# Gate and up in blocks of 128 features in both layers, and w_down in smaller pieces

## The chip, the cores and the metric

The kernel runs on one core of a Trainium2 chip. The metric is the device time of one execution in microseconds (us). Before the change three runs took 646.38, 647.87 and 648.17 us, median 647.87. The profile is of one further execution, which took 647.37 us.

The engines are named as in the profile: PE (matrix engine; PEld are its loads of the stationary operand), DVE, ACT, POOL, and SP, which here only issues transfers (DMA).

## The reference

One token for each of B = 4 sequences passes through two layers. Each layer is a block of attention over a cache and a feed-forward block, both on a normalised x and both added to x. The same caches and weights serve both layers.

```
x: [4, 1, 512]   k_cache, v_cache: [4, 8, 8192, 128]   wq: [512, 4096]   wo: [4096, 512]
w_gate, w_up: [512, 1792]   w_down: [1792, 512]          all bf16

twice:
  h = layernorm(x)
  q = h @ wq                      # 32 heads of 128; 4 query heads share one of 8 KV heads
  p = softmax(q k^T / sqrt(128))  # over 8192 keys
  x = x + (p v) @ wo
  h = layernorm(x)
  x = x + (silu(h @ w_gate) * (h @ w_up)) @ w_down
```

K and V are 64 MB each and are read in both layers, apart from a few pieces that are kept. With the weights, read in each layer or once, 271 MB come in.

## The kernel before, in words

**Tiles and slots.** One tile of K or V is 4 MB: two KV heads of one sequence, all 8192 keys, 32 KB on each of 128 partitions. `kvf` holds five slots of that size. `todo` runs over the 16 pairs of a layer: `keys` turns K by transposes on DVE (L581) and multiplies it with the queries (L607), `values` multiplies V with the probabilities (L745). All transfers go through SP in the order of the list `cmds`; `freed` marks places of a slot as free and `pump` issues the next transfers of the list as long as their place is free. Nothing else decides the order.

**Weights of the feed-forward block.** When attention nears its end, a slot that is free takes the weights (`W_SLOT`: slot 1 in layer 0, slot 3 in layer 1). w_gate has 4 passes of 128 input features (kt), each 1792 features wide; w_up the same, part of it in a place that stays for both layers. w_down is cut into ranges of 128-feature blocks, `WDS[L]`: five ranges in layer 0, three in layer 1. In layer 0 there is too little room: two ranges have a place (one in `pT`), and the other three go where gate passes 0, 1 and 2 were, each issued when its pass has been multiplied (`freed(s, NB + 2 + k, ...)`). In layer 1 two ranges are issued with gate and up, the third, blocks 12 and 13, when the last pair's probabilities (`late`) are no longer needed.

**Gate and up.** `ffn(L)` does gate in bank `gb`, then up in bank `ub`, pass by pass (wg0 to wg3, wu0 and wu1), and a small matmul for the variance (`deviation`, L931) after gate pass 1. The two layers differ:

- Layer 0: x is stationary (4 columns), the weights stream by. Each pass has four strips of FW = 448 features (`strips`), one for each quarter of the array, so that the results of sequence b lie on partitions 0, 32, 64 and 96 plus b. One strip of up is cut in two where its weights lie in two places: 33 matmuls in all. `on_end` (L1023) turns each bank by a transpose on DVE, and features come to lie on partitions. Feature p x 14 + f is then on partition p, and w_down is loaded to match: partition p holds rows p x 14 + f.
- Layer 1: the weights are stationary, 128 features a block, x streams by (4 columns): 14 blocks a pass, 112 in all. Results have features on partitions at once. `base(fo)` gives a block's first feature and the step between its features, so that they match the order in which w_down lies: for range j in groups of `WDE[j]` rows, a partition holds `WDE[j]` consecutive rows. `WDE = (8, 4, 2)`: the blocks of range 0 take every 8th feature, those of range 1 every 4th, of range 2 every 2nd.

**From there** DVE and ACT compute gate times its sigmoid (L1054 to L1060, the rstd of the norm is multiplied in) and times up (L1062), which gives hT in bf16. In layer 0 w_down follows with its blocks stationary (L1079), range by range as they land; in layer 1 hT is stationary and w_down streams by into four quarters of a bank (L1069), so that the result is in rows and can go out (L1144, L1146, L1148). `x_rows` (L907) adds x into the same bank. L912 to L926 (`center`) stand ahead of both: mean, xn, squares.

**Queries.** `qproj` (L996) uses quarters of the array as layer 0's gate and up do. The change leaves it as it is.

Of the kernel before, what the change touches and what calls it, by code (L numbers as in the profile page):

```python
# [6 lines left out]
ALU = mybir.AluOpType  # L7
# [96 lines left out]
def bass_interleave_layers__gqa_block_cached__swiglu_ffn__decode_kernel(  # L104
# [18 lines left out]
    P = 128  # L123
# [21 lines left out]
    with ExitStack() as es:  # L145
# [14 lines left out]
        WDS = (((12, 14), (10, 12), (0, 2), (2, 6), (6, 10)), ((0, 8), (8, 12), (12, 14)))  # L160
        WDE = (8, 4, 2)
        NW = max(len(w) for w in WDS)
# [24 lines left out]

        def base(fo):
            j = next(j for j, w in enumerate(WDS[1]) if w[0] <= fo < w[1])
            a, e = WDS[1][j][0], WDE[j]  # L190
            return a * P + (fo - a) // e * e * P + (fo - a) % e, e

        FW = F // NA
        assert FW * NA == F and FW == FO * QB and FW <= 512

# [4 lines left out]
        def wu_at(s, k, f, n, e=1):  # L200
            o = k * F + f
            o = (NSLOT + 1) * SL + o if o < RES else s * SL + O_WU + o - RES
            return kvf[:, o:o + e * (n - 1) + 1:e]

        def strips(up, k):
            for a in range(NA):
                cuts = [a * FW, (a + 1) * FW]
                if up and cuts[0] < RES - k * F < cuts[1]:
                    cuts.insert(1, RES - k * F)
                for f, end in zip(cuts, cuts[1:]):  # L210
                    yield a, f, end - f

# [270 lines left out]
        def load_wd(w0, L, j, also=()):  # L483
            a, b = WDS[L][j]
            o = 0 if w0 is pTf else wd_from(L, a)
            dst, src = w0[:, o:o + (b - a) * D], B_w_down.rearrange("(p f) n -> p (f n)", f=FO)[:, a * D:b * D]
            if L:
                dst = dst.rearrange("p (m x) -> p m x", x=WDE[j] * D)
                src = B_w_down[a * P:b * P, :].rearrange("(m p e) n -> p m (e n)", p=P, e=WDE[j])
            T.dma("sp", dst, src, sem_w["wd"][j], writes=[f"wd{j}"] + list(also))  # L490

# [519 lines left out]
        def ffn(L):  # L1011
# [3 lines left out]
            uT = bank(ub)[:, 0:FO * B]  # L1015
            fb = lambda ap: ap.rearrange("p (f b) -> p b f" if L else "p (b f) -> p b f", b=B)
            rb = rstd[:].unsqueeze(2).to_broadcast([P, B, FO])

            def on_end(k):
                if L:  # L1020
                    return
                blk = bank(k)[:, 0:FW].rearrange("p (i f) -> p f i", f=FO)
                T.op("dve", lambda e: e.transpose(blk, blk), reads=[f"pb{k}"], writes=[f"pb{k}"])  # L1023
            rooms = {"wg0": room(s, 0, F), "wg1": room(s, F, 2 * F), "wg2": room(s, 2 * F, 3 * F), "wg3": room(s, 3 * F, O_WU), "wu0": [], "wu1": room(s, O_WU, O_WD)}
# [4 lines left out]
            for wname, bk, ks in (("wg0", gb, (0, 1)), ("wg1", gb, (1, 2)),  # L1029
                                      ("wg2", gb, (2, 3)), ("wg3", gb, (3, KT)),  # L1030
                                      ("wu0", ub, (0, KT // 2)), ("wu1", ub, (KT // 2, KT))):
                at = wu_at if bk == ub else wg_at
                for kt in range(*ks):
                    parts = [(0, *base(fo), fo) for fo in range(FO)] if L else [(a, f, w, 0) for a, f, w in strips(bk == ub, kt)]
                    for n, (a, f, w, fo) in enumerate(parts):
                        x = xn[:, kt * B:(kt + 1) * B]
                        if L:
                            to, lhs, rhs = bank(bk)[:, fo * B:(fo + 1) * B], at(s, kt, f, P, w), x
                        else:
                            to, lhs, rhs = bank(bk)[a * QB:a * QB + B, f - a * FW:f - a * FW + w], x, at(s, kt, f, w)  # L1040
                        T.op("pe", lambda e: e.matmul(to, lhsT=lhs, rhs=rhs, start=(kt == 0 and fo == 0),  # L1041
                                                      stop=(kt == KT - 1 and (not L or fo == FO - 1))),
                             reads=rooms[wname] + names[wname] + ["xn"], writes=[f"pb{bk}"],
                             sig=(kt == ks[1] - 1 and n == len(parts) - 1))
                if wname in ("wg0", "wg1", "wg2"):
                    k = int(wname[2])
                    if not L:
                        freed(s, NB + 2 + k, NB + 3 + k)
                    if k == 1:
                        deviation(zero_sb, "zero", SBK[1])  # L1050
                elif wname != "wu0":
                    freed(s, *((0 if L else GATE, UP) if wname == "wg3" else (UP, DOWN)))
            on_end(gb)
            T.op("dve", lambda e: e.tensor_tensor(fb(gr), fb(gT), rb, ALU.mult),  # L1054
# [5 lines left out]
            T.op("dve", lambda e: e.tensor_tensor(eg, gw, eg, ALU.mult), reads=["gw", "eg"], writes=["eg"])  # L1060
            on_end(ub)
            T.op("dve", lambda e: e.tensor_tensor(hT.rearrange("p (f b) -> p b f", b=B), fb(eg), fb(uT), ALU.mult), reads=[f"pb{ub}", "eg"], writes=["hT"])  # L1062
            if L == 1:
# [114 lines left out]
```

## Time and profile before

| | |
|---|---|
| median of three runs | 647.87 us (646.38 to 648.17) |
| profiled execution | 647.37 us, span 645.1 us |
| PE busy | 414.8 us (64%) |
| PE weight loads busy | 172.3 us (27%) |
| DVE busy | 426.3 us (66%) |
| ACT, POOL busy | 50.2 us (8%), 11.9 us (2%) |
| DMA | 271.76 MB, mean 421 GB/s; queue 1: 98.8% of 16 engines |
| mean granted clock of PE | 0.841 |

How to read it: shares are of the span. The span is cut into 40 slices of 16.1 us; a digit is the busy share in tenths. Timeline lines give start and duration in us, engine, line of the kernel, operation, operands and how many instructions were merged; in brackets stands the idle time before and what ended it. A merged line's duration is from the first start to the last end, so that overlapping instructions are not counted twice. "DMA to landing" is the time from a transfer's issue to the arrival of its last part. The profiled execution's own time is 2.24 us more than its span.

### The profile page before, as it was taken

Reading aid. Unit: us, or ns where it says so; the run is one execution under the profiler, and the core shown is the slowest. Engines: PE = TensorE matmul, PEld = TensorE weight load, DVE = VectorE, ACT = ScalarE, POOL = GpSimd, SP = SyncE. Lnnn points to the kernel's source line nnn. Section 1 sums busy time; section 2 is a strip of 40 time slices with the busy share of each in tenths; the row PEclk is TensorE's granted clock in tenths of the full one; section 3 lists DMA queues with packets and bytes.
Section 4 is the critical chain, followed back from the end, with each engine's and each line's share of the span. In section 5 each row is a group of like instructions: output and inputs, shape, how many; then the busy total and the mean of one; then the engine's idle time right before and its main releaser. Section 6 shows DMA issues by size and latency. Waiting matters only on the chain.

```text
span 645.1 us, 6824 instructions
## 1 busy us (share of the span) xinstructions
PE 414.8 (64%) x2807; PEld 172.3 (27%) x2809; DVE 426.3 (66%) x599; ACT 50.2 (8%) x138; POOL 11.9 (2%) x44
## 2 busy tenths in 40 slices
PE   0583475457765746757856977667655567657867
PEld 0231122122222312322223332222222222223326
DVE  5375467456776656777853878967765557766953
ACT  0100000000000000000010300000000000000110
POOL 0000000000000000000000000000000000000000
PEclk9995887688876888778975999998777897679986
DMA  9999999999999999999999999999999999999995
GB/s 367 446 422 419 445 430 423 426 431 440 427 425 440 430 427 430 433 433 426 435 411 372 415 441 425 432 430 437 426 433 430 433 426 431 439 426 428 439 409 218
DMA packets 15502, 271.76 MB, mean 421 GB/s; under 512 B 1640, under 2 KB 1648, under 8 KB 6896
## 3 DMA queue, kind: packets, MB, share of 16 engines
q1 hardware_dynamic: 15472, 271.33, 98.8%
q8 instruction: 22, 0.36, 0.2%
q14 instruction: 8, 0.07, 0.0%
HBM read 271.32 MB, written 0.00 MB: 421 GB/s over the span
## 4 chain that ended last, share of the span: by engine, by line
DMA 60%; DVE 20%; PE 15%; issue 4%; ACT 0%; SPq 0%; POOL 0%; ACTq 0%; DVEq 0%; POOLq 0%
DMA kvf<-in_A_k_cache_dram 45%; DVE kvf L581 15%; DMA kvf<-in_A_v_cache_dram 11%; PE ps L607 8%; DMA kvf<-in_A_wq_dram 3%; PE ps L745 2%; DVE pb L797 2%; PE ps L1041 1%; DMA kvf<-in_B_w_down_dram 1%; PE ps L996 1%; DVE pT L673 1%; DVE pb L793 1%; DVE ps L547 0%; DVE scr L807 0%; PE ps L889 0%
## 5 line engine op out<-in xcount | busy, mean ns | idle before, releaser
L607 PE MATMUL ps<-kvf,zq 128*128 128x512 bf16 x1024 | 291.1, 430 | 186.0 <-DVE kvf L581 178.7
L581 DVE STREAM_TRANSPOSE kvf<-kvf 128x2048 f32<-128x2048 f32 (+1 forms) x133 | 280.5, 2132 | 125.4 <-DMA kvf<-in_A_k_cache_dram 125.2
L607 PEld LDWEIGHTS ps<-kvf,zq 128*128 128x128 bf16 x1024 | 98.7, 108 | 344.0 <-DVE kvf L581 223.6
L745 PE MATMUL ps<-kvf,pT 128*32 128x512 bf16 x960 | 65.8, 396 | 1.5 <-DVE pT L673 1.5
L655 ACT ACTIVATE pb<-ps,tiny 128x512 bf16<-128x512 f32 x32 | 24.9, 777 | 507.7 <-DVE tiny L653 489.2
L673 DVE STREAM_TRANSPOSE pT<-pb 64x512 bf16<-64x512 bf16 x60 | 41.2, 686 | 3.0 <-ACT pb L655 2.0
L797 DVE SCALAR_TENSOR_TENSOR pb<-ps,tiny,pb 128x128 f32<-128x128 f32 x104 | 36.5, 351 | 5.8 <-PE ps L745 2.1
L613 DVE TENSOR_REDUCE tiny<-ps 128x1 f32<-128x512 f32 x32 | 22.0, 688 | 20.7 <-PE ps L607 20.7
L745 PEld LDWEIGHTS ps<-kvf,pT 128*32 128x32 bf16 x960 | 20.8, 98 | 31.2 <-issue 14.8
L802 PEld LDWEIGHTS ps<-sel,pb 128*128 128x128 f32 x64 | 16.3, 263 | 16.0 <-DVE pb L797 7.9
L597 POOL TENSOR_TENSOR zq<-scr,tiny 128x64 bf16<-128x64 bf16 x30 | 9.2, 306 | 525.8 <-PE ps L607 525.8
L621 DVE TENSOR_REDUCE mrm<-ps 1x8 f32<-1x128 f32 x32 | 8.8, 273 | 13.5 <-PE ps L618 13.5
L802 PE MATMUL ps<-sel,pb 128*128 128x8 f32 x64 | 12.0, 260 | 5.1 <-DVE pb L797 5.1
L645 PEld LDWEIGHTS ps<-mrm,tiny 128*128 128x128 f32 x60 | 12.6, 215 | 9.0 <-issue 5.7
L996 PE MATMUL ps<-kvf,xn 128*4 128x512 bf16 x64 | 7.5, 621 | 11.1 <-DMA kvf<-in_A_wq_dram 10.8
L645 PE MATMUL ps<-mrm,tiny 128*128 128x16 f32 x60 | 9.8, 240 | 3.3 <-ACT mrm L658 3.3
L793 DVE TENSOR_SCALAR pb<-ps,tiny 128x128 f32<-128x128 f32 x32 | 10.1, 316 | 2.6 <-PE ps L745 2.6
L864 PE MATMUL ps<-wo_sb,scr 128*4 128x512 bf16 x48 | 10.8, 379 | 0.6 <-DVE scr L833 0.6
L658 ACT ACTIVATE mrm<-head,tiny 128x8 f32<-128x8 f32 x32 | 9.6, 301 | 1.0
L618 PE MATMUL ps<-identf,tiny 128*1 128x128 f32 x32 | 8.6, 270 | 1.2 <-DVE tiny L613 1.2
L807 DVE TENSOR_TENSOR scr<-ps,rl 128x8 bf16<-128x8 f32 x32 | 5.7, 177 | 3.2 <-PE ps L802 2.2
L745 PE MATMUL ps<-kvf 128*32 128x512 bf16 (+2 forms) x96 | 5.5, 361 | 3.4 <-DMA kvf<-in_A_v_cache_dram 3.3
(91 smaller groups left out, 121.5 us busy)
## 6 DMA issues: line engine op xcount, KB each, us to landing
kvf<-in_A_k_cache_dram SPq DMA_DIRECT2D x27, 4096.0 KB, 31.2
kvf<-in_A_v_cache_dram SPq DMA_DIRECT2D x27, 4096.0 KB, 34.5
kvf<-in_A_v_cache_dram SPq DMA_DIRECT2D x3, 2048.0 KB, 26.4
kvf<-in_A_k_cache_dram SPq DMA_DIRECT2D x11, 512.0 KB, 7.0
kvf<-in_A_k_cache_dram SPq DMA_DIRECT2D x2, 2048.0 KB, 9.4
kvf<-in_A_wq_dram SPq DMA_DIRECT2D x2, 2048.0 KB, 18.1
wo_sb<-in_A_wo_dram SPq DMA_DIRECT2D x4, 1024.0 KB, 41.5
kvf<-in_B_w_gate_dram SPq DMA_DIRECT2D x2, 1792.0 KB, 24.5
```

The lines of the kernel that those rows point to most:

```text
L581: T.op("dve", lambda e: e.transpose(w, w), reads=names, writes=names)
L607: T.op("pe", lambda e: e.matmul(bank(bk)[:, 0:SW], lhsT=zq[:, z0:z0 + P], rhs=w[:, :, c // 2, :, c % 2], start=(q == 0 and c == 0), stop=( ...
L613: T.op("dve", lambda e: e.tensor_reduce(mx[:], bank(bk)[:, 0:SW], AX.X, ALU.max), reads=[f"pb{bk}"], writes=["mx"])
L645: T.op("pe", lambda e: e.matmul(at, lhsT=ones, rhs=mrm[:, i * H2:(i + 2) * H2], start=True, stop=True), reads=[f"m8{i}", "rsm", "onesf"], ...
L655: T.op("act", lambda e: e.activation(pb[:], bank(bk)[:, 0:SW], ACTF.Exp, bias=nm, scale=rstd[:, b:b + 1], accum_out=rs), reads=[f"pb{bk}", ...
L673: T.op("dve", lambda e: e.transpose(dst, pb[hp]), reads=["pb", "row"], writes=[name])
L745: T.op("pe", lambda e: e.matmul(bank(k)[j * QB:(j + 1) * QB, q0 * Dh:q1 * Dh], lhsT=p_t[:, t, h, :], rhs=v[:, q0:q1, t, :], start=((last o ...
L793: T.op("dve", lambda e: e.tensor_scalar(into, o, own[:, q:q + 1], None, op0=ALU.mult), reads=[f"pb{k}", "own"], writes=["row"] if last els ...
L797: T.op("dve", lambda e: e.scalar_tensor_tensor(into, o, own[:, q:q + 1], into, op0=ALU.mult, op1=ALU.add), reads=[f"pb{k}", "own", iname], ...
L802: T.op("pe", lambda e: e.matmul(at, lhsT=into, rhs=sel[:], start=True, stop=True), reads=[iname, "sel"], writes=[name])
L864: T.op("pe", lambda e: e.matmul(bank(OUTB)[0:B, 0:D], lhsT=oT[:, o, :], rhs=wo_sb[:, h, :], start=(gp == groups[L][0] and r == 0), stop=(g ...
L996: T.op("pe", lambda e: e.matmul(bank(QK[k])[a * QB:a * QB + B, :], lhsT=xn[:, kt * B:(kt + 1) * B], rhs=wq_sb[:, kt, f:f + W2], start=(kt ...
```

## The change

Layer 0 gets the form that layer 1 has: blocks of 128 features stationary, x streaming by. Strips, the quarters of `ffn` and the transposes `on_end` go. w_down of layer 0 is loaded in the matching order. In both layers a block's features now are 2 or 4 apart: `WDE` becomes `((2, 2, 2, 4, 4), (2, 2, 2))`. For layer 0 the contiguous pieces keep their size, 2 KB for ranges of two blocks and 4 KB for ranges of four; only which rows lie on a partition changes. In layer 1 the first range (1 MB) goes from pieces of 8 KB to 2 KB, the second (512 KB) from 4 KB to 2 KB. The order of operands on DVE (`fb`, `rb`) follows the results' order, which now is the same in both layers. The transfers, their order and what frees their places stay.

```diff
-        WDE = (8, 4, 2)
+        WDE = ((2, 2, 2, 4, 4), (2, 2, 2))
...
-        def base(fo):
-            j = next(j for j, w in enumerate(WDS[1]) if w[0] <= fo < w[1])
-            a, e = WDS[1][j][0], WDE[j]
+        def base(L, fo):
+            j = next(j for j, w in enumerate(WDS[L]) if w[0] <= fo < w[1])
+            a, e = WDS[L][j][0], WDE[L][j]
             return a * P + (fo - a) // e * e * P + (fo - a) % e, e
-
-        FW = F // NA
-        assert FW * NA == F and FW == FO * QB and FW <= 512
...
-        def strips(up, k):
-            for a in range(NA):
-                cuts = [a * FW, (a + 1) * FW]
-                if up and cuts[0] < RES - k * F < cuts[1]:
-                    cuts.insert(1, RES - k * F)
-                for f, end in zip(cuts, cuts[1:]):
-                    yield a, f, end - f
...
         def load_wd(w0, L, j, also=()):
             a, b = WDS[L][j]
             o = 0 if w0 is pTf else wd_from(L, a)
-            dst, src = w0[:, o:o + (b - a) * D], B_w_down.rearrange("(p f) n -> p (f n)", f=FO)[:, a * D:b * D]
-            if L:
-                dst = dst.rearrange("p (m x) -> p m x", x=WDE[j] * D)
-                src = B_w_down[a * P:b * P, :].rearrange("(m p e) n -> p m (e n)", p=P, e=WDE[j])
-            T.dma("sp", dst, src, sem_w["wd"][j], writes=[f"wd{j}"] + list(also))
+            T.dma("sp", w0[:, o:o + (b - a) * D].rearrange("p (m x) -> p m x", x=WDE[L][j] * D),
+                  B_w_down[a * P:b * P, :].rearrange("(m p e) n -> p m (e n)", p=P, e=WDE[L][j]), sem_w["wd"][j], writes=[f"wd{j}"] + list(also))
...
-            fb = lambda ap: ap.rearrange("p (f b) -> p b f" if L else "p (b f) -> p b f", b=B)
-            rb = rstd[:].unsqueeze(2).to_broadcast([P, B, FO])
-
-            def on_end(k):
-                if L:
-                    return
-                blk = bank(k)[:, 0:FW].rearrange("p (i f) -> p f i", f=FO)
-                T.op("dve", lambda e: e.transpose(blk, blk), reads=[f"pb{k}"], writes=[f"pb{k}"])
+            fb = lambda ap: ap.rearrange("p (f b) -> p f b", b=B)
+            rb = rstd[:].unsqueeze(1).to_broadcast([P, FO, B])
...
                 for kt in range(*ks):
-                    parts = [(0, *base(fo), fo) for fo in range(FO)] if L else [(a, f, w, 0) for a, f, w in strips(bk == ub, kt)]
-                    for n, (a, f, w, fo) in enumerate(parts):
-                        x = xn[:, kt * B:(kt + 1) * B]
-                        if L:
-                            to, lhs, rhs = bank(bk)[:, fo * B:(fo + 1) * B], at(s, kt, f, P, w), x
-                        else:
-                            to, lhs, rhs = bank(bk)[a * QB:a * QB + B, f - a * FW:f - a * FW + w], x, at(s, kt, f, w)
-                        T.op("pe", lambda e: e.matmul(to, lhsT=lhs, rhs=rhs, start=(kt == 0 and fo == 0),
-                                                      stop=(kt == KT - 1 and (not L or fo == FO - 1))),
+                    for fo in range(FO):
+                        f, e_ = base(L, fo)
+                        T.op("pe", lambda e: e.matmul(bank(bk)[:, fo * B:(fo + 1) * B], lhsT=at(s, kt, f, P, e_),
+                                                      rhs=xn[:, kt * B:(kt + 1) * B],
+                                                      start=(kt == 0 and fo == 0), stop=(kt == KT - 1 and fo == FO - 1)),
                              reads=rooms[wname] + names[wname] + ["xn"], writes=[f"pb{bk}"],
-                             sig=(kt == ks[1] - 1 and n == len(parts) - 1))
+                             sig=(kt == ks[1] - 1 and fo == FO - 1))
...
-            on_end(gb)
             T.op("dve", lambda e: e.tensor_tensor(fb(gr), fb(gT), rb, ALU.mult),
                  reads=[f"pb{gb}", "rstd"], writes=["gr", "pb"])
...
-            on_end(ub)
-            T.op("dve", lambda e: e.tensor_tensor(hT.rearrange("p (f b) -> p b f", b=B), fb(eg), fb(uT), ALU.mult), reads=[f"pb{ub}", "eg"], writes=["hT"])
+            T.op("dve", lambda e: e.tensor_tensor(hT, eg, uT, ALU.mult), reads=[f"pb{ub}", "eg"], writes=["hT"])
```

## The prediction

> **What bounds the kernel now.** I read the page's slices and DMA queues first, then the timeline of the two feed-forward stages (layer 0 at 342 to 352 us, layer 1 at 634 to 645 us), then the times to landing of w_down.
>
> The page, whole run:
>
> ```profile
> span 645.1 us, 6824 instructions
> ...
> PEclk9995887688876888778975999998777897679986
> DMA  9999999999999999999999999999999999999995
> GB/s 367 446 422 419 445 430 423 426 431 440 427 425 440 430 427 430 433 433 426 435 411 372 415 441 425 432 430 437 426 433 430 433 426 431 439 426 428 439 409 218
> ...
> q1 hardware_dynamic: 15472, 271.33, 98.8%
> ```
>
> The sixteen DMA engines are full in every slice but the last, so up to the last V piece the time is bytes over bandwidth. The trace's landing records add that the engines do not finish together: of the last V piece the first engine's share lands at 626.30 us and the last engine's at 629.97. A consumer waits for the last one. I call that engine the late engine; its stream, not the mean, sets every wait on a DMA.
>
> The tail of layer 1 (start, duration, engine, line, instruction):
>
> ```profile
> 634.88 1.42 PEld L1041 LDWEIGHTS ps<-xn,kvf 128*128 128x128 bf16 x28 [0.22 <-issue]
> ...
> 636.46 4.30 PEld L1041 LDWEIGHTS ps<-xn,kvf 128*128 128x128 bf16 x84
> ...
> 638.19 0.27 DVE L1054 TENSOR_TENSOR pb<-ps,tiny 128x56 f32<-128x56 f32 x1 [3.00 <-PE ps L1041]
> ...
> 639.54 0.22 DVE L1060 TENSOR_TENSOR pb<-pb 128x56 f32<-128x56 f32 x1
> ...
> 640.88 0.28 DVE L1062 TENSOR_TENSOR pb<-pb,ps 128x56 bf16<-128x56 f32 x1 [1.13 <-PE ps L1041]
> ...
> 641.22 1.67 PE L1069 MATMUL ps<-kvf,pb 128*4 128x128 bf16 x56
> ...
> 643.58 0.29 SPq L1148 DMA_DIRECT2D out_dram<-pb  x1
> ```
>
> Gate (28 + 28 block matmuls) and up (56) of layer 1 already use blocks of 128 features as stationary operand. The up blocks end at 640.66, L1062 makes hT at 640.88, and only then does w_down (L1069) start. From there to the end of the span everything is serial. The three w_down transfers of that layer, issued at 604.79, 605.27 and 630.47:
>
> ```profile
> L93 SPq DMA_DIRECT2D kvf<-in_B_w_down_dram x3: 328/430/4178, 604.8 to 630.5; - x3
> ...
> DMA to landing us min/median/max: 10.3/34.1/34.8
> ```
>
> Issue plus time to landing: 638.85, 640.11 and 640.73 us. So the last weights are there 0.49 us before L1069 starts at 641.22: the end hangs on the PE chain, with a second chain only half a microsecond behind it.
>
> Layer 0, with four strips of 448 columns per pass:
>
> ```profile
> 342.85 0.92 PE L1041 MATMUL ps<-kvf,xn 128*4 128x448 bf16 x8 [0.36 <-DVE pb L922]
> ...
> 345.18 0.67 DVE L1023 STREAM_TRANSPOSE ps<-ps 128x448 f32<-128x448 f32 x1 [1.98 <-PE ps L1041]
> ...
> 346.34 0.91 PE L1041 MATMUL ps<-kvf,xn 128*4 128x448 bf16 x9 [0.47 <-DMA kvf<-in_B_w_up_dram]
> ...
> 347.31 0.67 DVE L1023 STREAM_TRANSPOSE ps<-ps 128x448 f32<-128x448 f32 x1
> 348.01 0.28 DVE L1062 TENSOR_TENSOR pb<-pb,ps 128x56 bf16<-128x56 f32 x1
> ...
> 350.73 0.59 PE L1079 MATMUL ps<-pb,kvf 128*128 128x4 bf16 x16 [0.65 <-DMA kvf<-in_B_w_down_dram]
> ```
>
> Up waits for its weights at 346.34, and the last w_down pieces come at 350.73. hT was ready at 348.29, 2.4 us earlier. Layer 0 is bound by DMA, not by gate, up or the two transposes L1023.
>
> **The change, part by part.**
>
> *1. Layer 1, step between a block's columns from 8 and 4 to 2.* The trace's single weight loads show the price. In each pass of 14 blocks the eight loads of columns 8 elements apart start 60 ns after one another; the four at step 4 and the two at step 2 start 31 ns apart at first, 27 ns at the end of the run; the 32 loads of L889 (step 2) take 0.87 us, 27 ns each. A pass takes 0.674 us now. At 27 ns it would take 0.374, at 31 ns 0.434; I take 27, since L889 and L1079 hold it over 32 and 16 loads. That is 0.30 us less per pass (0.24 at 31), and there are 8: 2.4 us of PE time (1.9). On the path: gate blocks start at 634.88 as before (xn is the wait, L919). Passes 1 and 2 end at 635.63; L931 needs the squares of L926 (done 635.19), so it moves up with them. The next load started 0.27 us after the last of pass 2, and the one after it 0.21 later, so passes 3 and 4 run to 636.83 and L1054, 0.23 us after the last load before, goes to about 637.05 instead of 638.19. rstd (L937, done 637.45) depends on L931 and comes at 636.9, in time. The chain L1054 to L1060 keeps its 1.57 us and ends at 638.62. Up ends at 638.33 by its loads, plus 0.22 to L1062. So L1062 starts at 638.65 instead of 640.88, and hT is there 2.2 us earlier, at 638.93. Now the gate chain on DVE is last, not up.
>
> *2. Layer 1, w_down in packets of 2 KB instead of 8 and 4.* The trace's packets last 313 ns at 8 KB, 159 at 4 KB and 84 at 2 KB (medians). Each engine has 8 packets of 8 KB and 8 of 4 KB; they become 32 and 16 of 2 KB: (32 x 84 - 8 x 313) + (16 x 84 - 8 x 159) = 184 + 72 = 0.26 us more. Before, 0.49 us of slack would hide it. With part 1 the slack is gone: first pieces land at 639.03, second at 640.37, last at 640.99.
>
> *3. What L1069 then does.* It takes 0.107 us per block of four strips (1.5 us over 14), at the granted clock of 0.50 that the windows show from 635 us on; I leave that as it is. Block 1 starts at 639.08 (weights), eight blocks end at 639.94; it waits for the second piece until 640.41, four blocks to 640.83; it waits for the last until 641.03; two blocks and the 0.31 us of the last matmul: 641.45. Before it was 642.88. **Gain 1.43 us**; the 2.25 us after it stay. Without weight waits it would end at 640.69: gain 2.19.
>
> *4. Layer 0: 112 blocks for 33 strips, two transposes out.* A pass of strips starts every 0.33 to 0.37 us; a pass of blocks takes 0.37 to 0.43. So the gate passes end 0 to 0.2 us later in sum, and the three w_down transfers that SP issues when passes 1, 2 and 3 free their place (343.49, 343.87, 344.80) go out that much later. On the late engine they queue behind pieces that land at 346.20, 346.88 and 347.53, and then come at 348.18, 349.45 and 350.69, spaced as their size at full rate; an output of 4 KB shows 1.27 us from issue to landing, so some 1.5 us of delay is covered. If that cover were gone, each microsecond would delay 350.73 by one. Queued behind on SP are the K pieces of layer 1 (345.50 on), with the same cover. After the up weights at 346.34 two passes take 0.86 against 0.91; without the second transpose (0.67) hT comes about 0.5 us earlier and waits for weights: L1079's last blocks still start at 350.73. The first transpose is before L1054, but the gate chain ends at 347.39 and the up transpose was the last: nothing either. Value 0, bounds -0.2 (the 0.82 busy DMA of the microsecond at 344 refilled) to +0.2.
>
> *5. DVE operands in plain order* (L1054, L1057, L1062): layer 1 shows 0.27, 0.27 and 0.28 us, layer 0 in its order 0.22, 0.22 and 0.28. Up to 0.1 us, on the DVE chain, which in step 3 is covered by the weights: 0. POOL and ACT get nothing new; SP issues as many transfers in the same order.
>
> **Sum:** -1.43 + 0 (bounds -2.3 and -0.6). The low end has the weights ahead of PE; the high end has the late engine 0.8 us later still (one 8 KB packet at 637.7 took 774 ns instead of 313, just after an instruction fetch of 1.1 us at 636.56; layer 0 has 158 more PE instructions, so the fetches fall elsewhere and another of that size is possible). The profiled execution took 647.37 us, 0.50 under the median of 647.87; from the median: **646.4**.
>
> One rule speaks against this. The Trainium skill, TensorE: Matmul & The Clock Gate, section LDWEIGHTS, gives a load as the number of columns over 1.2, whatever the step: an estimate of 107 ns for 128 columns, 12.0 us for 112 loads. The trace disagrees: 112 loads took 1.42 + 4.30 us. By the rule the step would bring nothing in layer 1 and layer 0's blocks would take 8.5 us more than the strips' 3.5 (0.92 + 1.66 + 0.91): the loss of rival D.
>
> **Rivals.**
>
> *A, the weights are ahead.* If the instruction fetch misses the late engine, w_down lands 0.5 us or more earlier than I put it and PE sets the end: gain 2.0 to 2.3 us, 645.6 to 645.9. For it: the late engine's lag over the first grew from 3.64 to 4.38 us only in the first w_down transfer. Against: that is the run we have.
>
> *B, the step is not what spaces the loads* (order within the pass, say, since the eight come first). Then L1062 does not move, the 0.26 us stay hidden: 647.9. Against: all eight passes show 60 then 31, whatever came before.
>
> *C, slower: SP's queue.* The second w_down transfer held SP 4.18 us (the maximum above), the other transfers of layer 1's weights under 0.5: the queue seems to have had no room. 24 + 8 more packets per engine must find room before the last 256 KB can be issued. By the late engine's landings (619.77 to 629.97) room comes at about 632 instead of 630.47; its turn at the engine is near 640.3, so that costs nothing. From an issue at about 636 on, each microsecond costs one; a loss of 2 us needs some 3.4 us more. Issued at 639.5 it would end near 650.
>
> *D, slower: layer 0's blocks do not overlap.* At the duration of one load from start to end (103 to 162 ns, least and median in layer 1) the three gate passes that free places take 4.3 to 6.8 us instead of 1.3 (four strips at 0.33); past the 1.5 us of cover that pushes the late engine back 1.5 to 4 us, and layer 1 still gains 1.4: 648 to 650.5. It turns the gain into a loss once the passes run 2.9 us longer (1.5 of cover and the 1.43). Against: 28 loads of the same form in 1.42 us.
>
> **How the numbers follow.** 0.3% is 1.94 us, about what a measurement of this kernel can tell from no change. Forecast 0.53: its range 645.8 to 647.3, of which 0.47 lies within 0.3% and 0.06 beyond. A 0.28, faster. B 0.09, the same. C and D 0.05 each, slower. So faster 0.34, same 0.56, slower 0.10. Range 645.4 to 648.0: from A's best to B, with C and D left out.
>
> **What would show it.** Right: 112 loads of layer 1 in some 3.6 us instead of 5.7; the last DVE step (L1062 before) 3.8 us after the first gate block instead of 6.0; w_down matmuls broken by one or two waits for w_down; layer 0's last w_down wait still within 0.3 us. Wrong: loads still 60 ns apart (B); w_down matmuls in one piece (A); SP's last weight issue after 636 (C); layer 0's w_down pieces late (D). A late engine that lags more or less than 4 us by chance would shift everything after it.

## The result, and the profile after

The changed kernel takes 645.47 us (median of 8 runs, 645.00 to 645.69); the kernel before, on the same chip, 647.36 us (8 runs, 646.38 to 648.41). The ratio is 0.9969, with a 95% interval of 0.9959 to 0.9980: 1.9 us faster by the medians. Two later comparisons gave 0.9971 (0.9961 to 0.9980) and 0.9965 (0.9953 to 0.9977). The forecast was 646.4 us. The time lies inside its range, but the kernel is measurably faster, which the forecast held less likely than no difference.

Line numbers of the changed kernel are about 26 lower: gate and up blocks are L1016 (L1041 before), the gate chain L1029 to L1035 (L1054 to L1060), hT L1036 (L1062), layer 1's w_down L1043 (L1069), layer 0's L1053 (L1079), `x_rows` L893 (L907).

The page of the changed kernel. Slices and DMA queues say what they said before: the DMA engines are full up to the last slice.

```profile
span 642.9 us, 6981 instructions
PEclk9995886688876898768975899998767987679987
DMA  9999999999999999999999999999999999999996
q1 hardware_dynamic: 15984, 271.33, 99.1%
q8 instruction: 22, 0.36, 0.2%
```

The last line matters below: 22 packets of 16 KB (0.36 MB) that bring instructions.

The tail of layer 1 in the timeline of the changed kernel (start, duration, engine, line, instruction; in brackets the idle time before it and what ended it):

```profile
634.18 0.83 PEld L1016 LDWEIGHTS ps<-xn,kvf 128*128 128x128 bf16 x28 [0.19 <-issue]
...
635.17 2.50 PEld L1016 LDWEIGHTS ps<-xn,kvf 128*128 128x128 bf16 x84
...
636.31 0.22 DVE L1029 TENSOR_TENSOR pb<-ps,tiny 128x56 f32<-128x56 f32 x1 [1.74 <-PE ps L1016]
...
637.60 0.22 DVE L1035 TENSOR_TENSOR pb<-pb 128x56 f32<-128x56 f32 x1
...
637.92 0.21 DVE L1036 TENSOR_TENSOR pb<-pb,ps 128x56 bf16<-128x56 f32 x1
...
638.19 1.34 PE L1043 MATMUL ps<-kvf,pb 128*4 128x128 bf16 x44
...
640.17 0.49 PE L1043 MATMUL ps<-kvf,pb 128*4 128x128 bf16 x12 [0.64 <-issue]
...
641.36 0.29 SPq L1122 DMA_DIRECT2D out_dram<-pb  x1
```

The 112 loads take 0.83 + 2.50 = 3.33 us instead of 1.42 + 4.30 = 5.72. hT (L1036) starts 3.74 us after the first gate block instead of 6.00. The w_down matmuls then come in two parts, with a hole before the last twelve; but what ended the hole is "issue", that is nothing in the profile, and not a DMA. The end of the w_down matmuls moved from 642.88 to 640.66 us, by 2.22. The first gate block moved too, from 634.88 to 634.18, before anything in layer 1 could have helped it.

SP's transfers of w_down by the line that issues them (duration in ns: least, median, most):

```profile
L93 SPq DMA_DIRECT2D kvf<-in_B_w_down_dram x7: 328/383/19803, 338.4 to 629.9; - x7
```

One issue held SP for 19.8 us (4.18 before). It was layer 1's second w_down transfer; the third went out at 629.86 instead of 630.47, 4.8 us after that issue had ended, and its last packet landed at 639.56 by the trace's landing records (640.73 before).

Layer 0 in the timeline of the changed kernel:

```profile
342.66 0.99 PE L1016 MATMUL ps<-xn,kvf 128*128 128x4 bf16 x28 [0.36 <-DVE pb L908]
...
346.34 0.97 PE L1016 MATMUL ps<-xn,kvf 128*128 128x4 bf16 x28 [0.56 <-DMA kvf<-in_B_w_up_dram]
...
347.35 0.21 DVE L1036 TENSOR_TENSOR pb<-pb,ps 128x56 bf16<-128x56 f32 x1 [0.86 <-PE ps L1016]
...
350.78 0.59 PE L1053 MATMUL ps<-pb,kvf 128*128 128x4 bf16 x16 [0.68 <-DMA kvf<-in_B_w_down_dram]
```

Up still waits until 346.34 for its weights, hT comes 0.66 us earlier, and the last w_down blocks start at 350.78 against 350.73.

### The profile page after: what moved, and what is told of

It is laid out like the page before. It is cut to its first block, busy times and chain, and to the rows that moved or that the text cites. A ratio compares the mean times of both kernels' runs of the same rounds, so it can differ in the third digit from the quotient of the medians.

```text
span 642.9 us, 6981 instructions
## 1 busy us (share of the span) xinstructions
PE 413.0 (64%) x2886; PEld 173.2 (27%) x2888; DVE 424.9 (66%) x597; ACT 50.2 (8%) x138; POOL 11.9 (2%) x44
## 4 chain that ended last, share of the span: by engine, by line
DMA 60%; DVE 19%; PE 16%; issue 4%; ACT 0%; SPq 0%; POOL 0%; ACTq 0%; DVEq 0%; POOLq 0%
DMA kvf<-in_A_k_cache_dram 45%; DVE kvf L567 14%; DMA kvf<-in_A_v_cache_dram 11%; PE ps L593 10%; DMA kvf<-in_A_wq_dram 3%; PE ps L731 2%; DVE pb L783 2%; DMA kvf<-in_B_w_down_dram 1%; PE ps L982 1%; PE ps L1016 1%; DVE pT L659 1%; DVE pb L779 0%; DVE ps L533 0%; DVE scr L793 0%; PE ps L875 0%
## 5 line engine op out<-in xcount | busy, mean ns | idle before, releaser
L779 DVE TENSOR_SCALAR pb<-ps,tiny 128x128 f32<-128x128 f32 x32 | 10.1, 316 | 2.6 <-PE ps L731 2.6
```

Source lines behind the costliest of these rows:

```text
L779: T.op("dve", lambda e: e.tensor_scalar(into, o, own[:, q:q + 1], None, op0=ALU.mult), reads=[f"pb{k}", "own"], writes=["row"] if last els ...
```

## The experiments

Several theories were open. **Steps**: layer 1's smaller step gives the gain, and w_down's packets take part of it back. **Layer 0**: the new blocks there give part of it. **Fetch**: where the 16 KB packets of instructions fall gives part of it, and makes the hole. Later **chance** joined them: one profile's numbers were taken for the kernel's. Each ratio is to the kernel before on the same chip (its medians there: 647.79 us for E1 to E4, 647.70 for E5 to E8, 647.50 for E9 to E12, 647.27 for E13 to E16).

### One layer at a time, and instructions shifted

**E1**, the kernel before with layer 1's steps alone:

```diff
-        WDE = (8, 4, 2)
+        WDE = (2, 2, 2)
```

> The kernel before with only layer 1's steps and w_down pieces changed (2 KB, step 2); layer 0 keeps strips and transposes. Steps theory (all of the gain is the closer loads of layer 1): as the changed kernel, 645.5. Fetch theory (part of the changed kernel's gain is that instruction fetches fall on other DMA engines, because layer 0 has 158 more PE instructions, and part is lost again in a stall of 0.9 us at an instruction fetch inside the last w_down matmuls): late engine's last V piece near 630.0 as before, no stall, last w_down piece about 641.0, end 645.9. Layer-0 theory (the transposes and strips were worth something): 646.3 or more.

Measured 645.51 us, ratio 0.9966 (0.9954 to 0.9979): all of the gain without layer 0's part, and with TensorE's instructions where the kernel before has them. The stall that the fetch theory ruled out is there all the same, 0.72 us among the `x_rows` matmuls. V's last packet landed at 629.26 us, but the first gate block came no earlier than before; the gain lies behind it:

```profile
634.95 0.80 PEld L1041 LDWEIGHTS ps<-xn,kvf 128*128 128x128 bf16 x28 [0.19 <-issue]
...
635.91 2.50 PEld L1041 LDWEIGHTS ps<-xn,kvf 128*128 128x128 bf16 x84
```

**E2**, the changed kernel with layer 1's steps as before:

```diff
-        WDE = ((2, 2, 2, 4, 4), (2, 2, 2))
+        WDE = ((2, 2, 2, 4, 4), (8, 4, 2))
```

> The changed kernel with layer 1's w_down back to pieces of 8, 4 and 2 KB and steps 8, 4 and 2. Steps theory: no gain, 647.4. Fetch theory: the last V piece lands 0.6 us earlier as in the changed kernel, the tail after it is as long as before: 646.8. Layer-0 theory: 646.0 or less.

Measured 646.71 us, 0.9984 (0.9976 to 0.9993). Small, but its interval does not hold 1, so layer 0 was not yet cleared; of the three theories the fetch theory's 646.8 is nearest.

**E3** and **E4** shift TensorE's instructions by 158 in the kernel before and by 98 in the changed one. The additional matmuls stand beside the softmax of layer 0; nothing reads them.

```diff
+        def pad(n):
+            for _ in range(n):
+                T.op("pe", lambda e: e.matmul(bank(TOT)[:, 0:B], lhsT=wo_sb[:, 0, 0:P], rhs=wo_sb[:, 0, 0:B], start=True, stop=True),
+                     reads=["wo0"], writes=[f"pb{TOT}"], sig=False)
...
+            if (L, u) == (0, 11):
+                pad(79)      # E3;  pad(49) in E4
```

> The kernel before with 79 small matmuls (158 PE instructions, as many as layer 0 gains by the change) into an unused bank in the middle of layer 0, where PE has idle time. Steps theory: 647.4. Fetch theory: the last V piece lands about 0.6 us earlier, 646.8.

> The changed kernel with 49 small matmuls (98 PE instructions, so that the whole shift against before is 256 instructions, one fetch of 16 KB) at the same place. Steps theory: no change, 645.5, and the gap of 0.94 us inside the last w_down matmuls stays where it is. Fetch theory: that gap goes from there and the end comes about 0.6 us earlier, 644.9, if the fetch that now falls before the up blocks has time.

E3: 647.07 us, 0.9989 (0.9980 to 0.9998), between the two theories. E4: 644.58 us, 0.9954 (0.9941 to 0.9966). In E4 the hole has left the w_down matmuls; it stands earlier now, among the `x_rows` matmuls:

```profile
637.45 0.37 PE L900 MATMUL ps<-identf,xT 128*4 128x64 f32 x3
638.33 0.38 PE L900 MATMUL ps<-identf,xT 128*4 128x64 f32 x4 [0.51 <-issue]
```

Its place in the instruction stream moved by the padding: 26 instructions from the end in the changed kernel, 124 in E4. So it does not belong to w_down. That is the fetch theory's point; whether it is worth time is for E8.

### Step and packet apart

**E5**, steps 4, 4, 2 in layer 1:

```diff
-        WDE = ((2, 2, 2, 4, 4), (2, 2, 2))
+        WDE = ((2, 2, 2, 4, 4), (4, 4, 2))
```

> The changed kernel with layer 1's first w_down piece in 4 KB packets and its features 4 apart (steps 4, 4, 2 in place of 2, 2, 2). Steps theory (the load's time goes by the step, and 8 is slow): step 4 is as fast as 2, all 112 gate and up loads of layer 1 take 27 to 31 ns, hT comes 3.7 to 3.9 us after the first gate block, and the 0.13 us that 4 KB packets save in the first piece is too little to see: 645.2 to 645.7 us. Rival (each doubling of the step costs): the 64 loads of the first eight blocks stand near 45 ns, hT comes 1 us later, 645.9 to 646.4. The instruction count is that of the changed kernel, so the gap of 0.9 us in the w_down matmuls should stay.

645.61 us, 0.9974 (0.9963 to 0.9985). The loads start 33 ns apart, which neither theory said (27 to 31, or 45), and so in every block, those of step 2 too; 26 to 27 in the changed kernel. The first w_down matmul comes 4.52 us after the first gate block (4.01 in the changed kernel). Step 4 costs a little more than step 2, far less than step 8. The hole that was expected to stay is not there.

**E6** and **E7** take the two apart: the transfer gets a list of its own. In both, the rows of w_down are not those of the features that they meet; the two kernels leave that match out, which changes values only.

```diff
+        WLE = (WDE[0], (8, 4, 2))            # E6; (2, 2, 2) in E7, with (8, 4, 2) for layer 1 in WDE
...
-            T.dma("sp", w0[:, o:o + (b - a) * D].rearrange("p (m x) -> p m x", x=WDE[L][j] * D),
-                  B_w_down[a * P:b * P, :].rearrange("(m p e) n -> p m (e n)", p=P, e=WDE[L][j]), ...
+            T.dma("sp", w0[:, o:o + (b - a) * D].rearrange("p (m x) -> p m x", x=WLE[L][j] * D),
+                  B_w_down[a * P:b * P, :].rearrange("(m p e) n -> p m (e n)", p=P, e=WLE[L][j]), ...
```

> The changed kernel with layer 1's w_down loaded in packets of 16, 8 and 4 KB as before, and gate and up still by steps of 2: the w_down rows then do not belong to the features they are multiplied with, which changes values only. This is the packets' price alone. My sum's step 2: the 2 KB packets cost 0.26 us, so the last w_down piece should land 0.26 us earlier after the last V piece than in the changed kernel (10.19 us there), the end hardly moves as long as the gap in the w_down matmuls stays: 645.2 to 645.6 us. Rival (packets cost nothing on this engine): no change in the landings beyond 0.1 us, 645.3 to 645.7.

> The changed kernel with layer 1's w_down loaded in 4 KB packets (features by 2), and gate and up computed by steps of 8, 4 and 2 as before: again the w_down rows do not belong to the features they meet, which changes values only. This is the step's price alone. Steps theory: 64 of the 112 loads at 60 ns, 5.7 us for the loads, hT 2.2 to 2.3 us later than in the changed kernel after the first gate block, and the end set by TensorE rather than by w_down: 646.7 to 647.3 us. Rival (packets are the cause): as the changed kernel, 645.3 to 645.7.

E6, small steps with large packets: 645.01 us, 0.9964 (0.9950 to 0.9977). Its last w_down packet landed 9.96 us after the last of V, against 10.19 in the changed kernel: 0.23 us, where the prediction's step 2 had 0.26. This compares two single profiles, and that time scatters: with the small packets it was 10.12 to 10.22 in five profiles (the changed kernel, E16, E4, E8, E11) and 10.57 to 11.66 in four more (E13, E10, E1, E7), with the large ones 9.93 to 10.07 in four (E3, E6, E15, E9) and 10.23 to 10.76 in three (E14, E2, the kernel before). The lowest values lie 0.19 us apart. There was no hole, and the w_down matmuls ran in one piece:

```profile
639.06 1.66 PE L1044 MATMUL ps<-kvf,pb 128*4 128x128 bf16 x56
```

E7, large steps with small packets: 646.66 us, 0.9987 (0.9978 to 0.9995), and the loads are back at 1.44 + 4.30 us:

```profile
633.78 1.44 PEld L1017 LDWEIGHTS ps<-xn,kvf 128*128 128x128 bf16 x28 [0.19 <-issue]
...
635.39 4.30 PEld L1017 LDWEIGHTS ps<-xn,kvf 128*128 128x128 bf16 x84
```

So the step alone makes the loads fast, and the packets seem to cost about what their sizes say. Step 8 showed 58 to 63 ns for most loads within a pass, step 4 after it 30 to 33, step 2 26 to 28. The Trainium skill, SBUF — State Buffer, section Specifications (TRN2), gives 16-byte lines and asks for two hits in each for full bandwidth. In bf16 a step of 8 makes one hit, 4 makes two, 2 makes four; the measured order agrees with that, with the jump between 4 and 8.

### The hole

**E8**, as E4 with `pad(107)`: the last instruction boundary lies 240 from the end, where TensorE takes longer for 256 instructions.

> The changed kernel with 107 additional small matmuls (214 instructions) beside the softmax of layer 0's last group but four, which only shifts where TensorE's 16 KB pieces of instructions begin: the last boundary then lies 240 instructions from the end, and in the changed kernel TensorE takes 6.5 us for the 256 before it, more than the 4.6 to 5.7 us that a fetch took. Fetch theory: no gap over 0.3 us in TensorE's last stage, the w_down matmuls end 0.1 us after the last piece has landed, at 640.0 to 640.2 us for a landing as in the changed kernel, so 644.6 to 645.1 us. Rival (the gap is something else, tied to the place in the program): a gap of 0.7 to 0.9 us stays at the w_down matmuls or before x_rows, 645.3 to 645.9.

645.27 us, 0.9964 (0.9951 to 0.9976). The hole is gone, as the fetch theory said:

```profile
639.82 1.66 PE L1050 MATMUL ps<-kvf,pb 128*4 128x128 bf16 x56
```

But the time was not: 644.6 to 645.1 had been expected, and no difference from the changed kernel can be told. In this profile the first gate block came only at 635.85, 5.99 us after the last of V (4.81 in the changed kernel). TensorE was late: its granted clock in the windows was 0.50 from 606 to 608 us, where the changed kernel has 1.00, and from 612 us on it ran 2.3 us behind the changed kernel's profile until V's last pieces. So this one profile does not show what the hole is worth.

All profiles together say what the hole is. The trace's records of the instruction queue show a packet of 16 KB, running for 1.0 to 1.1 us in the cases below, for each 256 TensorE instructions (22 packets in the changed kernel). Here is the instruction that begins a new group of 256, the last such in the kernel or, for E11, one in layer 0:

```
                        packet starts   instruction runs   after   idle before it
the changed kernel          637.57          640.16          2.59       0.94
its second profile, E10     637.15          639.57          2.41       0.32
its third, E16              637.53          640.06          2.53       0.72
E13                         638.42          640.84          2.42       0.95
E1                          636.68          639.21          2.53       0.72
E4                          635.87          638.33          2.46       0.82
E11                         349.00          351.60          2.60       2.85
E5                          638.01          640.63          2.62       none
E6                          636.83          640.08          3.25       none
E8                          633.44          637.79          4.34       none
the kernel before           636.56          640.84          4.28       none
```

Idle is counted here from start to start. None of these groups was begun sooner than 2.4 us after its packet started, and every hole ends 2.4 to 2.6 us after it. In the holes of layer 1, TensorE had begun the group before 4.1 to 5.1 us ahead of that instruction; in the kernel before it took 6.8 us for as many instructions. Faster loads use instructions faster: that is how the change made the hole. Speed alone does not decide it. E6 has the changed kernel's loads and no hole, since its packet started 0.4 us after the group before was begun instead of 1.7 to 2.0; what sets that delay was not shown. The Trainium skill, Runtime: NRT & Kernel Launch, section Instruction fetch mechanics, has the blocks of 256 instructions and calls the crossing mostly hidden; the runs agree on the 256, and here the crossing is not hidden.

### Chance, and layer 0's cover

**E9** is the kernel before and **E10** the changed kernel, both unedited, with a profile of their own.

> The kernel before, unedited, profiled and timed as if it were a variant. It tells how much of the differences between profiles is the execution and not the kernel. Chance theory: the last piece of V lands anywhere from 629.0 to 630.2 us, as it did in the five profiles whose instructions are the same up to there (628.98, 629.23, 629.37, 629.87, 630.21), the first gate block comes 4.8 to 6.0 us after it, the ratio to the kernel before is within 0.05% of 1. Rival (V landing at 629.97 belongs to the kernel before): it lands within 0.2 us of that again.

> The changed kernel, unedited, a second profile beside the others of this call. Chance theory: V lands anywhere from 629.0 to 630.2 us rather than at 629.37 again, and the last w_down piece 10.0 to 10.3 us after it (up to 10.8 where an instruction fetch falls among its packets). Fetch theory: the gap of 0.6 to 1.0 us in TensorE's last stage is there again at the same instruction, 26 from the end. 645.2 to 645.7 us.

E9: 647.63 us, 1.0002 (0.9993 to 1.0010). E10: 645.47 us, 0.9971 (0.9961 to 0.9980). V's last packet landed at 629.81 in E9, within 0.2 us of 629.97, as the rival said, but at 628.98 in E10 (629.37 before). What differs in E9 is w_down: the last packet 10.07 us after V's, not 10.76. In the profile that the prediction used, a packet of instructions at 636.56 seems to have held the late engine, whose lag grew to 4.32 us; in E9 there was one at 636.3 too, but the late engine's lag stayed at 3.2. The hole in E10 is shorter than expected, 0.32 us. E10's waits between 637 and 641 us name both things that can hold the w_down matmuls, a third of a microsecond each:

```profile
PEld ps L1043 <- DMA kvf<-in_B_w_down_dram: 0.3, 1, 0.3
PEld ps L1043 <- issue: 0.3, 1, 0.3
```

**E11**, E8's 107 matmuls moved into layer 0's feed-forward stage:

```diff
+                if not L and wname == "wu1":
+                    pad(107, SBK[1])        # second argument: the bank
```

> The changed kernel with the 107 small matmuls placed among layer 0's gate and up blocks, ahead of the second half of up, instead of beside the softmax: 2.9 us of TensorE work at 26 to 27 ns each, where my prediction counted 1.5 us of cover. Layer 0's hT comes 2.3 us later, its w_down matmuls end 1.0 to 1.4 us later (352.4 to 352.8 us in place of 351.4). Cover theory: the K products that follow wait for their pieces anyway, so the whole takes as long as with the padding beside the softmax (644.6 to 645.4 us). Rival (layer 0's blocks are on the path): 0.8 to 1.2 us longer, 645.8 to 646.6.

649.44 us, ratio 1.0037 (1.0024 to 1.0050). Both theories missed: it lies 4.0 us above the upper end of the cover theory's time, 2.8 above its rival's. The timeline of E11:

```profile
345.35 2.99 PE L716 MATMUL ps<-wo_sb 128*128 128x4 bf16 x107
348.20 0.72 PE L1023 MATMUL ps<-xn,kvf 128*128 128x4 bf16 x19
351.60 0.41 PE L1023 MATMUL ps<-xn,kvf 128*128 128x4 bf16 x9 [2.68 <-issue]
```

To the 2.99 us of padding came a hole of 2.68 us, the longest of all, for the same reason: so many short instructions that the next group had not come. And SP stood still for it. Its issues at that place, first in E11, then in the changed kernel:

```profile
344.66 8.38 SPq L93 DMA_DIRECT2D kvf<-in_A_k_cache_dram  x3
```

```profile
344.96 3.40 SPq L93 DMA_DIRECT2D kvf<-in_A_k_cache_dram  x3
```

The second and third K piece of layer 1 go where up's weights were and can be issued only when up is done: from 352.04 us on instead of 347.35, 4.7 us later. They landed 2.7 us later (355.97 and 356.58 against 353.29 and 353.92), the two pieces after them 4.0 and 4.1 us later; the median is 4.2 us above E8's. So layer 0's up is on the path through the place it frees: of its 4.7 us of delay 2.0 were covered for these two pieces, and only some 0.5 in the whole time.

**E12**, E5's steps with E8's padding, the best version that the runs had pointed to:

> The changed kernel with steps 4, 4, 2 in layer 1 and the 107 additional small matmuls: the best version that the runs so far point to. The last w_down piece lands 10.0 to 10.1 us after the last of V instead of 10.2, no gap over 0.3 us in TensorE's last stage, and the w_down matmuls end 0.5 to 0.9 us after the last landing: 644.5 to 645.2 us. Rival (no gain from either): as the changed kernel, 645.3 to 645.7.

645.36 us, 0.9967 (0.9955 to 0.9978): no hole, loads 33 ns apart, the last w_down piece 10.33 us after V instead of the 10.0 to 10.1 expected, no gain over the changed kernel. E4's 0.9954 is the lowest ratio of all, but its interval overlaps those of the changed kernel. No version was shown to beat it.

### The square

**E13** (the kernel before with steps of 2 and `pad(79)`), **E14** (E3 again), **E15** (E2 again) and **E16** (the changed kernel) have the same number of TensorE instructions and ran on one chip.

> The kernel before with steps of 2 in layer 1 and 79 small matmuls (158 instructions) beside the softmax of layer 0's last group but four: layer 0 by strips, layer 1 as in the changed kernel, and the changed kernel's number of instructions. Layer-1 theory (layer 0 is worth nothing): as the changed kernel in this call, within 0.3 us, 645.2 to 645.7. Layer-0 theory (its blocks bring 0.5 to 1 us): that much slower than the changed kernel, 645.9 to 646.5.

> The kernel before with the 79 small matmuls alone, again: both layers as before. Layer-1 theory: within 0.4 us of the kernel before, 647.0 to 647.8. Shift theory (moving the instructions brings the V stream's end forward): 0.5 to 1 us faster than the kernel before, as in the first call.

> The changed kernel with layer 1 back at steps of 8, 4 and 2, again: layer 0 by blocks, layer 1 as before. Layer-1 theory: within 0.3 us of the padded kernel before, and 1.5 to 2.2 us slower than the changed kernel. Layer-0 theory: 0.5 to 1 us faster than the padded kernel before.

> The changed kernel, third profile: the square's fourth corner. Both theories: 645.2 to 645.8 us; the gap at the instruction 26 from the end is there, 0.3 to 1.0 us long by the time at which the packet with the next instructions ran.

Medians: E13 645.67, E14 646.58, E15 647.29, E16 645.37 us. The ratios as a square:

```
ratio to the kernel before       layer 1: steps 8, 4, 2             layer 1: steps of 2
layer 0 by strips           E14  0.9988 (0.9979 to 0.9998)     E13  0.9969 (0.9958 to 0.9981)
layer 0 by blocks           E15  0.9997 (0.9989 to 1.0005)     E16  0.9965 (0.9953 to 0.9977)
```

Down a column, layer 0's blocks are worth +0.09% and -0.04%: nothing that intervals of 0.1% each way can tell. Along a row, layer 1's steps are worth -0.19% and -0.32%, on average 0.26% or 1.65 us; E1, without padding, gave 0.34%. E14 came out 0.69 us under the kernel before, as the shift theory said; E15 lies 0.71 us above E14, which neither theory said. E13 has the changed kernel's hole, 0.95 us at the same instruction, without layer 0's blocks: the shift of the stream by 158 instructions puts it there, and the fast loads make it. L1076 are its w_down matmuls:

```profile
640.84 0.49 PE L1076 MATMUL ps<-kvf,pb 128*4 128x128 bf16 x12 [0.64 <-issue]
```

## Why the prediction was wrong, step by step

**Step 1, the loads: right.** 3.33 us against the 3.6 forecast, 26 to 27 ns a load, L1036 3.74 us after the first gate block against 3.8. E7 shows that the step alone does it. Rival B fell with that. So did the 107 ns a load by the section LDWEIGHTS of the Trainium skill's page TensorE: Matmul & The Clock Gate. Another section of that page, Weight-path perf modes — Fast Weight Load (FWL) and DoubleRow, has 128 columns of bf16 read in four parallel chunks of 32; by the same formula that is an estimate of 27 ns, and the loads at step 2 agree with it.

**Step 2, the packets: right as far as it was measured.** 0.26 us by their sizes, 0.23 between the profiles of E6 and the changed kernel, 0.19 between the lowest values of all profiles.

**Step 3, the wait for w_down: nearly the right size, wrong in cause.** The prediction broke L1069 by waits for the second and third piece and put the time from its first matmul to its end 0.71 us longer. In the three profiles of the changed kernel it is 2.47, 2.05 and 2.24 us where E6 and E8 took 1.66 without any wait: 0.81, 0.39 and 0.58 longer. But in two of them the wait is for instructions, in E10 for instructions and the last piece, half each. "Block 1 starts at 639.08 (weights)" failed too: the first piece landed at 637.50 to 637.75, before hT, and the matmuls started as soon as hT was there, at 638.04 to 638.31. The pieces landed sooner after V than I put them (the last after 10.19, 10.69 and 10.20 us instead of 11.02, my 640.99 less 629.97), since I carried over from the profile of before a delay that its second profile (10.07) does not have. The hole, which I had not seen coming, took most of that error's place in the sum.

**Two steps failed: step 3's landings of w_down, and "gate blocks start at 634.88 as before".** The sum came to 1.43 us of gain, and the three comparisons of the two kernels gave 1.9 to 2.0. The terms, in us:

```
                                    predicted   profile of after   mean of three after less mean of two before
first gate block                       0            -0.70              -0.74   (634.17 less 634.92)
from there to the first w_down         -2.14        -2.33              -2.35   (4.01 less 6.36)
from there to its last one's end       +0.71        +0.81              +0.59   (2.25 less 1.66)
sum                                    -1.43        -2.22              -2.50
```

The last two lines are layer 1's own. They were forecast at -1.43 and come to -1.76: 0.21 us because hT was there 0.1 us sooner (step 5) and the first w_down matmul did not wait for weights, 0.12 because the stops between the w_down matmuls were shorter on average than the waits that I had put there. The timed runs give layer 1's steps 1.65 us on average in the square (1.2 and 2.1), and 2.3 in E1. So the mechanism was right, and its gain was undersized by some 0.2 to 0.3 us or more.

The first line had no term in the sum. It cannot be the kernel's in full, since with it the profiles show some 0.5 us more than the timed runs. The first gate block follows V's last packet by 4.8 to 5.2 us in most profiles, and that packet landed anywhere from 628.98 to 630.21 us in eight profiles whose instructions up to there are the same (the changed kernel three times, E2, E5, E6, E7, E15). With the instructions of the kernel before it scatters as well: 629.97, 629.81, and 629.26 in E1. The means of the two groups, 629.44 and 629.68, lie closer together than the profiles within either. The prediction named that chance ("a late engine that lags more or less than 4 us by chance would shift everything") and gave it no term.

How much of the line is the kernel's stays open. For a part of the kernel's: four of the five runs with layer 1's steps as before and shifted or changed instructions ahead of it (E2, E3, E7, E14) lie 0.11 to 0.16% under the kernel before with intervals that do not hold 1, the fifth (E15) 0.03%, while the kernel before against itself gave +0.02%. Against it: E1 has no shift, its first gate block came at 634.95 us (late after V, in a profile with a low clock at 606 us), and its ratio is that of the changed kernel. Something near 0.1%, or 0.7 us, may come with a shift of the instructions; that it does, and how, was not shown.

A gain of 1.43 us lay under the 1.94 that I had set as the bound of "same"; the measured one lies on it.

**Step 4, layer 0: right, on a thinner reason than it had.** Worth nothing (the square; E1). But its cover was argued from the w_down pieces alone. E11 shows what limits it: K's next pieces, which wait on SP for up's place. In the changed kernel they go out when they did before (347.35 and 347.30 us), because up's end is set by its own weights in both.

**Step 5, the order on DVE: the sizes right, the cover not.** L1029 and L1032 now take 0.22 us, as layer 0's did, and hT (L1036) 0.21 instead of 0.28. The forecast put this at nothing because the weights would come later than hT. They came sooner, so it lies on the path: the first w_down matmul starts 4.01 us after the first gate block, and 4.12 in E13, which has the same loads and the old order. Whether it shortens the end was not shown, since in both the hole follows.

**Rivals.** A, the weights ahead and TensorE setting the end, comes nearest by its time (645.6 to 645.9); its picture, w_down in one piece, is E6's and E8's, not the changed kernel's. C's mechanism was there in full, 19.8 us of it; it fell where nothing behind it was late, since the third transfer waits for `late` at 629.9 anyway. D's was made to happen in E11: layer 0's up ended 4.7 us later, and that cost 4.2.

## What to carry to other kernels

A stationary operand of bf16 whose columns lie 8 elements apart loaded here at half the pace of one at step 2 (60 ns against 27): order the features so that blocks take steps of 2 or 4, and pay for it with shorter packets. When a chain of short instructions is made faster, look at the instruction queue next: here TensorE began no group of 256 sooner than 2.4 us after its packet had started. And take the landing of the last packet from several profiles before a sum hangs on it: it scattered over 1.2 us here, more than the forecast missed by.

## What the runs showed of the hardware that was not expected

- TensorE stopped for instructions in a straight run without branches: 0.3 to 0.95 us in layer 1, 2.68 us in E11. In layer 1's holes the packet started 1.7 to 2.6 us after the group before it was begun, while w_down was still coming in, and 2.4 to 2.6 us more passed until the new group ran.
- Loads at steps 4, 4, 2 ran at 33 ns in all blocks, those of step 2 as well (E5, E12); with steps 2, 2, 2 at 26 to 27 ns in all.
- The granted TensorE clock fell to 0.50 from 606 to 608 us in E1, E3 and E8 and stayed at 1.00 there in the changed kernel (0.85 in E5). In those three profiles the first gate block came 5.5 to 6.0 us after the last of V, in the others 4.8 to 5.2.
- An issue on SP's queue can stand for 19.8 us with nothing lost, when what stands behind it is not needed sooner.
